# Reordering four places of a hand-written schedule: a crossbar transpose, a scaling, a key transpose and a Strassen sum

## The chip, the core and the metric

The kernel runs on one core of a Trainium2 chip. The metric is the device time of one execution in microseconds (us); lower is better. One profiled execution gives the trace that all the durations below come from.

## What is computed

Eight batches go through causal attention with a sliding window of 64 positions, and the result goes through a layer norm and a two-layer feed-forward block with a residual connection. Cut to what matters:

```python
q, k, v: (8 batches, 8 heads, 576 positions, 64)  float32
scores = q @ k.T / 8;  mask: 0 <= pos_q - pos_k < 64
attn   = softmax(scores);  x = attn @ v        # (8, 576, 512), heads side by side
xn = (x - mean(x)) / sqrt(var(x) + 1e-6) * g_ln
out = x + relu(xn @ w_ch1) @ w_ch2             # w_ch1 512x2048, w_ch2 2048x512
```

## The kernel before

**Groups.** Each of groups 0 to 7 takes the first 512 positions of one batch; group 8 takes the last 64 positions of all eight. A group's 512 rows are four blocks of 128. In the names, `(g, kb)` is block `kb` of batch or group `g`.

**The feed-forward part of a group** is a list of *units* (`mlp_units`), run in order. Group 1 and group 2 begin with 16 units of the first layer in halves (`l1_half`, PSUM tile `hph`, L634): units 0 to 7 make columns 0 to 255 and read blocks 0 and 1 of the transposed input `zT`, units 8 to 15 make columns 256 to 511 and read blocks 2 and 3. Each unit's result leaves PSUM by a Relu on ScalarE (ACT, L639), and the pool `mm` that holds it has two banks. Then come 14 units of the second layer, in the Winograd form of Strassen's algorithm: seven products on TensorE (PE, L567), in the order 4, 1, 2, 6, 5, 7, 3, two units each, accumulated in the banks `pA`, `pB` and `pC`. The sums that the products read (`s_sums`, tiles `sS`, L541) and the adds of finished banks to the residual `xn` (`post`, L576 and L580) run on VectorE (DVE). Groups 3 to 7 take the first layer at full width (`hps`, L493).

**The next batch's attention** is laid between these units by hand. `at(i, f, ...)` puts a step into slot `i`, which runs after unit `i`; steps of one slot run in the order in which they were put there:

```python
for i, u in enumerate(units):
    u()
    for f, a in slots[i]:
        f(*a)
```

The program order decides everything: each engine and each DMA queue works through its own instructions in this order, and waits only for data, for a buffer, or for a place among the DMAs in flight.

**Steps that the change and the prediction touch**, in the order in which a block meets them:
- `cast_qk`, `cast_v` (L154, L182): float32 to half precision on GpSimd (POOL).
- `t_main(b, x, half)`: transposes q (`x` = 0) or k (`x` = 1) into `qkT`. For batch 2 by TensorE (L276), with the result copied out of PSUM by ScalarE (q, L257) or VectorE (k, L259). From batch 3 on, q goes by a DMA transpose through the crossbar on the sync queue (SP, L265).
- `part_vB`: two DMAs on SP that lay the value rows out a second time, shifted by 64 rows, after `cast_v`.
- `s_pe`, `s_exp`, `s_mask`: scores on TensorE (L349), exponentials on ScalarE (L359), mask on VectorE (L369). `first_scores(b, i)` puts those of blocks 0 and 1 in slots `i` to `i + 2`. `half` of `t_main` is heads 0 to 3 or 4 to 7.
- `b_pe`: probabilities times values on TensorE (L396). `b_rows`: reciprocal, product, statistics and aggregate on VectorE (L412, L416, L418, L421).
- `z_step`: the reciprocal root of the variance and the shifted mean, three small GpSimd instructions (L440 to L442). From group 3 on a fourth GpSimd instruction scales the block (L446); for batches 1 and 2 `z_act` (ScalarE, L452) or `z_dve` (VectorE, L456) does that later.
- `zt_step(g, kb)`: transposes the scaled block into `zT`. For batch 1 by TensorE (L470) with a ScalarE copy (L473), from batch 2 on by a DMA transpose on SP (L466).
- `load_qk`, `load_v`, `load_tail` (L92, L176, L104 to L106) load the batch after next and the tails; `store` (L528) writes results. All are on SP.

Of the kernel before, what the change touches and what calls it, by code (L numbers as in the profile page):

```python
# [13 lines left out]
ALU = mybir.AluOpType  # L14
# [4 lines left out]
def kernel(  # L19
# [10 lines left out]
    nc = tc.nc  # L30
# [49 lines left out]
    x_norm, zT, mvg, zsd, rstd = {}, {}, {}, {}, {}  # L80
# [367 lines left out]
    rsnm = {}  # L448

    def z_act(g, kb):  # L450
        rs, nm = rsnm[(g, kb)]
        nc.scalar.activation(out=zsd[(g, kb)], in_=x_norm[(g, kb // 2)][:, kb % 2, :], func=AF.Identity,  # L452
                             bias=nm, scale=rs)

    def z_dve(g, kb):
        nc.vector.tensor_scalar(out=zsd[(g, kb)], in0=x_norm[(g, kb // 2)][:, kb % 2, :],  # L456
                                scalar1=mvg[g][:, kb, 0:1], scalar2=rsnm[(g, kb)][0],
                                op0=ALU.subtract, op1=ALU.mult)
# [379 lines left out]
    for i in range(8):  # L838
# [8 lines left out]
        out=mask[0:64], in_=mask[0:64], compare_op=ALU.is_gt, fill=0.0,  # L847
# [3 lines left out]
        out=mask[64:128], in_=mask[64:128], compare_op=ALU.is_ge, fill=0.0,  # L851
# [87 lines left out]
    for g in range(NGRP):  # L939
# [4 lines left out]
        units, s_sums = mlp_units(g, (8, 16, 16)[g] if g < 3 else 0, g == 0, g > 0)  # L944
        slots = [[] for _ in range(len(units) + 1)]

        def at(i, f, *a):
            slots[min(i, len(slots) - 1)].append((f, a))

        def first_scores(b, i):  # L950
            at(i, s_pe, b, 0)
            at(i, s_pe, b, 1, False, "xps")
            at(i, s_exp, b, 0, 0, 1)
            at(i + 1, s_exp, b, 1, 0, 1)
            at(i + 1, s_mask, b, 0)
            at(i + 2, s_mask, b, 1)

        b = g + 1
        if g == 0:
# [19 lines left out]
            at(22, z_step, 1, 0)  # L979
            at(22, cast_act, 1, 0, 1)  # L980
            at(22, z_act, 1, 0)
            at(22, cast_qk, 1, 1, (1,))
            at(22, load_qk, 2, 1)
# [21 lines left out]
        if g == 1:  # L1005
            at(0, cast_qk, 2, 0, (0,))
            at(0, after_mask, 1, 3)
            at(0, cast_qk, 2, 0, (1,))
            at(0, cast_qk, 2, 1, (0,))
            at(0, alloc_v, 2)  # L1010
            at(0, alloc_qkT, 2)
            at(1, t_main, 2, 0, 0)
            at(1, b_pe, 1, 2, "t")
            at(1, b_pe, 1, 3, "sc")
            at(1, b_rows, 1, 2)
            at(1, z_step, 1, 2)
            at(1, cast_qk, 2, 1, (1,))
            at(1, b_rows, 1, 3)
            at(1, z_step, 1, 3)
            at(2, z_dve, 1, 2)  # L1020
            at(3, t_main, 2, 1, 0)
            at(4, t_main, 2, 0, 1)
            at(4, z_dve, 1, 3)
            for c in (0, 2):
                at(4, cast_v, 2, c, c + 2)
                at(5, part_vB, 2, c)
            at(5, zt_step, 1, 2)
            at(5, t_main, 2, 1, 1)
            at(6, zt_step, 1, 3)
            for n, i in enumerate((3, 2, 4)):  # L1030
                at(7, w2_sums, i, 4, 8)
            at(8, s_pe, 2, 0)
            at(8, s_pe, 2, 1, False, "xps")
            at(8, s_exp, 2, 0, 0, 1)
            at(9, s_mask, 2, 0)
            at(9, w2_sums, 1, 0, 8)
            at(10, s_exp, 2, 1, 0)
            at(11, s_exp, 2, 1, 1)
            at(12, s_sums, 0, 4, 1, 2)
            at(12, s_mask, 2, 1)  # L1040
            at(16, s_sums, 4, 8, 1, 2)
            at(20, s_sums, 0, 8, 3)
            at(24, s_sums, 0, 8, 4)
            for j in range(4):
                i = (13, 16, 22, 22)[j]
                at(i, b_pe, 2, j, "sc" if j == 3 else "xps")
                if j < 2:
                    at(i, s_mm, 2, j + 2)
                    at(19, s_mask, 2, j + 2)
                i = (13, 17, 23, 26)[j]  # L1050
                at(i, b_rows, 2, j)
                at(i, z_step, 2, j)
                if j < 3:
                    at((17, 20, 26)[j], z_act, 2, j)
                    at((17, 20, 26)[j], zt_step, 2, j)
            at(6, load_qk, 3, 0)
            at(8, load_qk, 3, 1)
            at(10, load_v, 3, 0, 4)
            at(8, alloc_qkT, 3)
            at(8, cast_qk, 3, 0)  # L1060
            at(14, cast_qk, 3, 1, (0,))
            at(17, cast_qk, 3, 1, (1,))
            at(18, alloc_v, 3)
            at(18, cast_v, 3, 0, 2)
            at(18, cast_v, 3, 2, 4)
            at(21, part_vB, 3, 0, 4)
            first_scores(3, 28)
            for i, (x, half) in zip((12, 21, 18, 24), ((0, 0), (1, 0), (0, 1), (1, 1))):
                at(i, t_main, 3, x, half, 0)
        if g == 2:  # L1070
            at(2, z_act, 2, 3)
            at(3, zt_step, 2, 3)
            at(3, load_qk, 4, 0)
            at(3, load_qk, 4, 1)
            at(3, load_v, 4, 0, 2)
        if g > 1 and b < B:
            tail = TAILS.get(g)
            at(2, b_pe, b, 0)
            at(2, b_rows, b, 0)
            at(2, z_step, b, 0)  # L1080
            at(2, s_pe, b, 2)
            at(2, s_exp, b, 2, 0, 1)
            at(3, s_mask, b, 2)
            if tail:
                r, i = NGRP - 1, tail[0]
                at(2, s_pe, r, i, False, "t")
                at(4, s_exp, r, i, 0)
                at(5, s_exp, r, i, 1)
                at(5, s_mask, r, i)
                at(7, b_pe, b, 1)  # L1090
                at(7, b_pe, r, i, "t")
                at(7, s_mm, b, 3)
                at(7, b_rows, b, 1)
                at(7, z_step, b, 1)
                at(8, s_mask, b, 3)
                at(8, b_rows, r, i)
                at(9, z_step, r, i)
                at(12, b_pe, b, 2)
                at(12, b_pe, b, 3, "sc")
                at(16, zt_step, r, i)  # L1100
            else:
                at(2, s_pe, b, 3, False, "t")
                at(4, s_exp, b, 3, 0)
                at(5, s_exp, b, 3, 1)
                at(5, s_mask, b, 3)
                at(7, b_pe, b, 1)
                at(7, b_pe, b, 2, "t")
                at(7, b_pe, b, 3, "sc")
                at(7, b_rows, b, 1)
                at(7, z_step, b, 1)  # L1110
            if g + 2 < B:
                at(5, alloc_qkT, g + 2)
                at(5, after_mask, *((NGRP - 1, tail[0]) if tail else (b, 3)))
                at(5, cast_qk, g + 2, 0)
                at(5, cast_qk, g + 2, 1, (0,))
                at(11, cast_qk, g + 2, 1, (1,))
            for j, i in ((2, 8 if g == 2 else 12), (3, 10 if g == 2 else 19)):
                at(i, b_rows, b, j)
                at(i, z_step, b, j)
            for j in range(4):  # L1120
                at((2, 14, 18, {3: 25, 5: 25}.get(b, 23))[j], zt_step, b, j)
        for n, i in enumerate(TAILS.get(g, ()) if b >= B else ()):
            ts = (13, 13, 17, 22) if n else (1, 2, 5, 11)
            at(ts[0], s_mm, NGRP - 1, i)
# [84 lines left out]
```

## Time and profile before

| | |
|---|---|
| time, median of 3 runs (lowest to highest) | 308.82 us (308.58 to 309.03) |
| the profiled execution | 308.97 us |
| its span | 307.2 us |
| TensorE busy | 292.8 us (95%) |
| VectorE busy | 220.1 us (72%) |
| GpSimd busy | 163.4 us (53%) |
| ScalarE busy | 154.7 us (50%) |
| 16 DMA engines, mean share of SP's queue | 78.7% |

How to read the views: a timeline line gives start, length, engine, source line, operation, output and inputs, how often, and in brackets the idle time before it with what ended it. A line of waits names the waiting engine and its source line, then what released it, then the total, the number and the longest. The chain of waits is the work that ended last, followed back step by step. PEld is TensorE's weight load, and `SPq` is an instruction of the sync queue that issues a DMA. In this execution group 1 begins at 53.6 us, group 2 at 88.8 and group 3 at 127.9.

### The profile page before, as it was taken

To read this page: it belongs to the slowest core of one execution; us is meant where nothing else is said; L and a number is where in the kernel's file an instruction comes from. 1 tells how busy PE (TensorE), PEld (TensorE's weight loads), DVE (VectorE), ACT (ScalarE), POOL (GpSimd) and SP (SyncE) were. 2 spreads that over 40 slices of the span, in tenths; PEclk is the share of its full clock that TensorE was granted. 3 is DMA by queue.
4 is the path that set the end of the run, shared out by engine and by line. 5 is a ranking of instruction groups with operands and counts; after the bars stand their busy time and mean duration, and the time that the engine had idled before them with its cause. 6 is when DMAs were issued, how large, how long until landed. Compare 5 with 4: busy or idle time off the path is not lost.

```text
span 307.2 us, 7809 instructions
## 1 busy us (share of the span) xinstructions
PE 292.8 (95%) x3179; PEld 207.1 (67%) x3179; DVE 220.1 (72%) x413; ACT 154.7 (50%) x260; POOL 163.4 (53%) x243
## 2 busy tenths in 40 slices
PE   8989999999997797999999999999999999999993
PEld 3657545888876686655975597559755864688882
DVE  3880387989986492459956985599558876689982
ACT  3566637686457342686247626862476046405500
POOL 4678887735833289059914963499127607024300
PEclk9999999999999799999999999999999999999999
DMA  8999999969943899799669998994629398003014
GB/s 189 262 385 337 388 280 294 267 204 302 143 123 113 250 221 170 202 316 202 94 178 321 175 197 234 316 152 100 135 101 188 70 168 209 17 19 139 1 36 104
DMA packets 114311, 58.36 MB, mean 190 GB/s; under 512 B 83682, under 2 KB 105250, under 8 KB 114275
## 3 DMA queue, kind: packets, MB, share of 16 engines
q1 hardware_dynamic: 113840, 57.47, 78.7%
q8 instruction: 25, 0.41, 0.6%
q10 hardware_dynamic: 434, 0.40, 0.4%
q14 instruction: 12, 0.09, 0.1%
HBM read 38.80 MB, written 9.44 MB: 157 GB/s over the span
## 4 chain that ended last, share of the span: by engine, by line
PE 77%; DVE 8%; SPq 6%; DMA 4%; POOL 2%; issue 1%; ACT 1%; DVEq 0%; POOLq 0%
PE hps L493 25%; PE pA L567 11%; PE pB L567 8%; PE pC L567 7%; PE hph L634 6%; PE ch L651 3%; PE xps L396 3%; PE sc L349 3%; SPq L176 2%; PE lA L690 2%; PE warm L861 2%; PE tp L276 2%; DVE xn L416 2%; DVE stats L418 2%; DMA tk<-in_k_dram 1%
## 5 line engine op out<-in xcount | busy, mean ns | idle before, releaser
L493 PE MATMUL hps<-zT,w1g 128*128 128x512 f16 x352 | 80.2, 379 | 0.4 <-DMA zT<-z 0.4
L497 ACT ACTIVATE hrT<-hps 128x512 f16<-128x512 f32 x88 | 52.8, 600 | 37.3 <-PE hps L493 34.2
L493 PEld LDWEIGHTS <-w1g 128*128 128x128 f16 x352 | 33.1, 98 | 38.6 <-issue 1.7
L567 PEld LDWEIGHTS <-sS 128*128 128x128 f16 x512 | 49.4, 98 | 6.2 <-issue 0.5
L359 ACT ACTIVATE pt<-sc 128x512 f16<-128x512 f32 x72 | 39.3, 601 | 20.3 <-PE sc L349 19.7
L440 POOL TENSOR_SCALAR rsz<-mvg 128x1 f32<-128x1 f32 x32 | 11.2, 350 | 66.3 <-DVE mvg L421 59.1
L634 PE MATMUL hph<-zT,w1g 128*128 128x256 f16 x320 | 39.3, 280 | 3.6 <-DMA zT<-z 3.5
L154 POOL CAST qk<-qk 128x1024 f16<-128x1024 f32 x29 | 32.7, 1142 | 16.6 <-DMA qk<-in_q_dram 14.3
L567 PEld LDWEIGHTS <-hrT 128*128 128x128 f16 x384 | 36.7, 98 | 7.0 <-ACT hrT L497 0.8
L634 PEld LDWEIGHTS <-w1g 128*128 128x128 f16 x320 | 31.3, 100 | 8.8 <-DMA zT<-z 3.6
L369 DVE TENSOR_TENSOR pt<-pt,mask 128x1024 f16<-128x1024 f16 x32 | 23.7, 748 | 17.9 <-ACT pt L359 17.9
L639 ACT ACTIVATE hrT<-hph 128x512 f16<-128x512 f32 x40 | 23.9, 599 | 16.2 <-PE hph L634 16.0
L541 DVE TENSOR_TENSOR sS<-hrT 128x1024 f16<-128x1024 f16 (+2 forms) x41 | 26.6, 648 | 7.1 <-ACT hrT L639 5.2
L567 PE MATMUL pC<-w2s,sS 128*128 128x256 f16 x256 | 31.1, 273 | 0.3 <-DVE xn L580 0.3
L567 PE MATMUL pA<-wT,sS 128*128 128x256 f16 x256 | 30.9, 273 | 0.0
L257 ACT COPY qkT<-tp 128x1024 f16<-128x1024 f16 (+1 forms) x18 | 17.3, 962 | 25.0 <-PE tp L276 23.2
L416 DVE TENSOR_TENSOR xn<-xps,rcp 128x256 f32<-128x256 f32 (+1 forms) x50 | 25.8, 539 | 2.4 <-DMA out_dram<-xn 1.6
L418 DVE BATCH_NORM_STATS2 stats<-xn 128x6 f32<-128x512 f32 x36 | 25.0, 695 | 1.2
L446 POOL TENSOR_SCALAR z<-xn,rsz 128x512 f16<-128x512 f32 x24 | 22.2, 927 | 2.5
L441 POOL TENSOR_TENSOR rsz<-rsz,mhalf 128x1 f32<-128x1 f32 x32 | 20.6, 642 | 2.7
L182 POOL CAST vA<-v 128x1024 f16<-128x1024 f32 (+1 forms) x18 | 16.0, 906 | 4.4 <-DMA v<-in_v_dram 4.2
L396 PEld LDWEIGHTS <-pt 128*64 128x64 f16 x576 | 11.5, 110 | 9.1 <-issue 5.1
(120 smaller groups left out, 420.4 us busy)
## 6 DMA issues: line engine op xcount, KB each, us to landing
qk<-in_q_dram SPq DMA_DIRECT2D x16, 512.0 KB, 5.9
qk<-in_k_dram SPq DMA_DIRECT2D x16, 512.0 KB, 6.8
out_dram<-xn SPq DMA_DIRECT2D x32, 256.0 KB, 3.4
v<-in_v_dram SPq DMA_DIRECT2D x28, 256.0 KB, 6.6
w2s<-in_moe_w_ch_dram SPq DMA_DIRECT2D x9, 512.0 KB, 8.5
w1s<-in_moe_w_ch_dram SPq DMA_DIRECT2D x4, 512.0 KB, 7.2
tk<-in_k_dram SPq DMA_DIRECT2D x8, 256.0 KB, 4.8
tv<-in_v_dram SPq DMA_DIRECT2D x8, 256.0 KB, 5.1
```

Of the source, the lines that this page charges most:

```text
L154: nc.gpsimd.tensor_copy(out=dst[:, :].rearrange("p (a j) e d -> p a e j d", j=j), in_=t[:, :].rearrange("p (a e j d) -> p a e j d", e=2, j ...
L359: nc.scalar.activation(out=o, in_=i, func=AF.Exp, bias=0.0, scale=scale)
L369: nc.vector.tensor_tensor(out=ptv, in0=ptv, in1=mb, op=ALU.mult)
L416: nc.vector.tensor_tensor(out=xn[:, n * i:n * i + n], in0=xps[:, :, 0:D], in1=rcp_b, op=ALU.mult)
L418: nc.vector.bn_stats(out=stats, in_=xv)
L446: nc.gpsimd.tensor_scalar(out=z, in0=xv, scalar1=rs, scalar2=nm, op0=ALU.mult, op1=ALU.add)
L493: nc.tensor.matmul(out=hps, lhsT=w1g[:, kc, 128 * hc:128 * (hc + 1)], rhs=zT[g][:, kc, :], start=(kc == 0), stop=(kc == NKC - 1),)
L497: nc.scalar.activation(out=hrT[:, hc, :], in_=hps, func=AF.Relu, bias=0.0, scale=1.0)
L541: nc.vector.tensor_tensor(out=o, in0=x, in1=y, op=op)
L567: nc.tensor.matmul(out=o, lhsT=a[:, c, 128 * p:128 * p + 128], rhs=wv[:, c, :], start=(first and (p == 0 or split_c) and c == 0), stop=(c ...
L634: nc.tensor.matmul(out=hps[:, e], lhsT=w1g[:, kc, 128 * hc:128 * (hc + 1)], rhs=zT[g][:, kc, 256 * half:256 * half + 256], start=(kc == 0) ...
L639: nc.scalar.activation(out=hrT[:, 2 * i:2 * i + 2, 256 * half:256 * half + 256], in_=hps, func=AF.Relu, bias=0.0, scale=1.0)
```

## The change

Four places in groups 1 and 2 move:

1. In group 2, batch 3's block 0 is transposed through the crossbar in slot 4 instead of slot 2, and batch 2's block 3 in slot 2 instead of slot 3. On the sync queue batch 2's block now stands ahead of batch 4's loads (four of q and k, four of v), and batch 3's block behind them and ahead of the tail loads. Before, batch 3's block came first, batch 2's second, and then the loads.
2. In group 1, batch 1's block 3 is scaled by a new step `z_pool` on GpSimd right after its small steps, where `z_dve` did it on VectorE in slot 4. The cast of the second half of batch 2's k, which stood on GpSimd between blocks 2 and 3, follows the scaling.
3. In group 1, TensorE's transposes of the second half of batch 2's k go from slot 5 to slot 8, directly ahead of batch 2's first scores. VectorE's copy of them goes behind the three w2 sums.
4. At the end of group 1, the fourth sum `sS` and the adds of product banks A and C come ahead of the value rows of batch 2's block 2 on VectorE, and batch 3's first scores on TensorE come behind both units of product 3 instead of between them.

ScalarE's order is the same as before. TensorE has the same instructions, VectorE one fewer and GpSimd one more.

```diff
+    def z_pool(g, kb):
+        rs, nm = rsnm[(g, kb)]
+        nc.gpsimd.tensor_scalar(out=zsd[(g, kb)], in0=x_norm[(g, kb // 2)][:, kb % 2, :], scalar1=rs, scalar2=nm,
+                                op0=ALU.mult, op1=ALU.add)
...
         if g == 1:
...
             at(1, z_step, 1, 2)
-            at(1, cast_qk, 2, 1, (1,))
             at(1, b_rows, 1, 3)
             at(1, z_step, 1, 3)
+            at(1, z_pool, 1, 3)
+            at(1, cast_qk, 2, 1, (1,))
             at(2, z_dve, 1, 2)
             at(3, t_main, 2, 1, 0)
             at(4, t_main, 2, 0, 1)
-            at(4, z_dve, 1, 3)
...
             at(5, zt_step, 1, 2)
-            at(5, t_main, 2, 1, 1)
             at(6, zt_step, 1, 3)
+            at(8, t_main, 2, 1, 1)
...
             at(8, s_pe, 2, 0)
...
-            at(24, s_sums, 0, 8, 4)
+            at(22, s_sums, 0, 8, 4)
...
-                i = (13, 17, 23, 26)[j]
+                i = (13, 17, 25, 25)[j]
                 at(i, b_rows, 2, j)
                 at(i, z_step, 2, j)
...
-            first_scores(3, 28)
+            first_scores(3, 29)
...
         if g == 2:
             at(2, z_act, 2, 3)
-            at(3, zt_step, 2, 3)
+            at(2, zt_step, 2, 3)
             at(3, load_qk, 4, 0)
...
             for j in range(4):
-                at((2, 14, 18, {3: 25, 5: 25}.get(b, 23))[j], zt_step, b, j)
+                at((4 if g == 2 else 2, 14, 18, {3: 25, 5: 25}.get(b, 23))[j], zt_step, b, j)
```

## The prediction, made before the changed kernel was run

> **What bounds the kernel now.** I read the page's busy shares first: TensorE (PE) is busy 292.8 of 307.2 us, so only its 14.4 us of idle time and any slow-clocked stretch are there to be won. Next I read the waits of TensorE alone between 50 and 130 us (waiting engine and line, releaser: total us, times, longest):
>
> ```profile
> PE hph L634 <- DMA zT<-z: 3.5, 1, 3.5
> PE tp L276 <- POOL qk L154: 1.8, 1, 1.8
> PE hps L493 <- DMA zT<-z: 0.4, 1, 0.4
> PE pC L567 <- DVE xn L580: 0.3, 1, 0.3
> PE ztp L470 <- DVE z L456: 0.3, 1, 0.3
> PE sc L349 <- DMA qkT<-qk: 0.2, 1, 0.2
> ```
>
> One wait stands out: group 2's half-width first-layer products (hph) stop for a transposed block zT. The timeline of all engines around it (start, length, what) shows why:
>
> ```profile
> 92.11 0.80 ACT L452 ACTIVATE z<-xn,rsz 128x512 f16<-128x512 f32 x1
> ...
> 96.75 1.20 POOL L446 TENSOR_SCALAR z<-xn,rsz 128x512 f16<-128x512 f32 x1
> ...
> 97.97 2.51 SPq L466 DMA_TRANSPOSE zT<-z  x2
> ...
> 100.54 0.57 SPq L92 DMA_DIRECT2D qk<-in_q_dram  x1
> ...
> 101.64 8.77 PE L634 MATMUL hph<-zT,w1g 128*128 128x256 f16 x64 [3.54 <-DMA zT<-z]
> ```
>
> Batch 2's last block is scaled on ScalarE by 92.91, but the sync queue (SP) first holds the transpose of batch 3's block 0, whose GpSimd scaling ends at 97.95. So batch 2's transpose issues at 99.27 and lands near 101.6, and batch 4's loads start only at 100.54. The stall costs more than its length, as hph's stages show (us; PE busy; ACT busy; granted clock; DMA share; GB/s):
>
> ```profile
> 98.10:101.64 3.54, 0.00 (x0) 0.00 (x0) 0.99 0.33 74
> 101.64:103.50 1.86, 1.86 (x9) 0.00 (x0) 0.50 0.79 189
> 103.50:105.20 1.70, 1.70 (x11) 0.60 (x1) 0.57 1.05 365
> 106.10:110.20 4.10, 4.10 (x40) 2.96 (x5) 1.00 1.20 302
> ```
>
> After the idle 3.54 us the clock is half for about 3.5 us. The 64 matmuls took 8.61 us to the next one's start at 110.25; at 1.75 per 16, as in group 1, they take 7.00. That is another 1.61.
>
> **The swap of the two transposes.** At 92.24 the queue has issued its four stores and is idle. With batch 2's block first, it issues right behind ScalarE: one transpose issue is 1.21, landing is 2.4 after the start. The stall would go, and batch 4's loads would move from 100.54 to about 92.95 + 1.21 + 0.06 = 94.2, or 6.3 earlier, if group 1 and the start of group 2 kept their times. They do not; that is the next two parts.
>
> Batch 3's block 0 now issues behind four qk and four v loads, still ahead of the tail loads. Its reader is group 3 at 127.9, so its own landing is harmless; the question is what its place costs the queue. Later groups have this order already (the sync queue's timeline):
>
> ```profile
> 160.85 0.46 SPq L92 DMA_DIRECT2D qk<-in_q_dram  x1
> ...
> 167.17 3.10 SPq L466 DMA_TRANSPOSE zT<-z  x1
> ...
> 178.76 3.84 SPq L265 DMA_TRANSPOSE qkT<-qk  x2
> ```
>
> There, first load to first qkT transpose is 17.91, with such a block inside; in group 2 the same eight plus six loads take 118.51 - 100.54 = 17.97 without one. Engines are full there (DMA share 1.05 from 101.6 to 110), so the issue hides in the backlog. I take 0, and 1.2 (one issue) as the other end.
>
> **Group 1: scaling on GpSimd, k's second half later.** The chain of waits carries this place:
>
> ```profile
> 61.90 1.19 DVE z L456
> ...
> 63.13 0.40 PE ztp L470 x4
> 63.53 1.75 PE hph L634 x16
> 65.28 0.57 PE sc L349 x32
> ...
> 84.59 1.11 DVE sS L541
> 85.70 0.60 DVE xn L580
> ```
>
> Now block 3's three small GpSimd steps start behind VectorE's aggregate (end 59.96, plus the 0.16 lag of block 2's), take 1.25 as at 60.57, and the scaling follows 0.1 later at 61.45. Its rows (L446) are 0.76 alone and 1.21 beside VectorE's half-precision sums; the three w2 sums (0.69 each) run from 61.9. So it ends at 62.2 to 62.7, against 63.08 on VectorE. TensorE, with the eight k transposes (0.45) taken out ahead, wants it at 62.2: it waits 0.3, the same as now. The longest such row, 2.17, would add 1.0.
>
> [...]
>
> The k transposes now stand directly ahead of batch 2's first scores, and those read what they produce: heads 0 to 3 are ready, heads 4 to 7 wait for VectorE's copy (1.21 for this tile) plus 0.2 from TensorE's end to VectorE's start and 0.05 back. The first eight of 32 score matmuls cover 0.57 / 4 = 0.14. New wait: 1.32. Queued behind it are the exponentials and the rest of half 1, and TensorE is then busy without a gap to 84 (6.00 of 6.00 in three stages), so nothing absorbs it. Call it 1.3 (1.1 to 2.3).
>
> GpSimd does batch 2's k and v casts about 1.7 later (z and cast order), and SP waits at 62.82 and 64.12 for them, so vB and batch 3's loads go 1.7 later, 0.4 more than TensorE does. The nearest one, batch 3's value cast, has no slack (its last load lands at about 83.1 and the cast starts then); what follows on GpSimd, block 2's small steps, comes 2.2 later anyway. I count 0. That VectorE loses a scaling (1.2) is worth 0: it then waits for TensorE.
>
> **End of group 1: the fourth sum and the C add ahead of the rows.** Gain: TensorE's 0.34 before the last C product goes, since VectorE's add of the first C product (end 84.11 on TensorE, plus 0.2, 0.6 long) is over at 84.9 while product 7 runs to 86.02. Cost: block 2's rows start at 84.9, not 82.72. They take 1.87, ending 86.8 instead of 84.59. GpSimd's small steps then take 1.35 (as for block 3; 2.2 as now beside the sum is the other end), so ScalarE scales block 2 at 88.13 instead of 86.79 and is done at 88.94. ScalarE runs in order: behind it queue batch 3's four exponentials (87.82 now, 2.06 long) and the first Relu of group 2 (89.90 now, releasing a bank at 90.50 that TensorE takes at 90.53 for its third product). The exponentials start at about 88.97, 1.15 later (1.1 to 2.0); the Relu and the third product follow. The scores, one slot later, pay only for 0.1: block 3's rows leave their bank at 87.85. From there ScalarE is the pace: 7.10 busy of 8.20 us between 90.0 and 98.2.
>
> **The sum.** Half 0 of group 2 runs 1.3 + 1.15 = 2.45 late (2.2 to 3.6). Block 3's scaling ends at 92.91 + 2.45 = 95.36, its transpose issues 95.4 to 96.6 and lands at 97.8, well before TensorE arrives at 100.55: no stall, full clock. TensorE is then 1.1 ahead of before, and 2.7 ahead after half 1. Batch 4's loads start at 96.65, 3.9 earlier. The next late thing is their chain. The cast of k's second half (ends 118.79 now, behind casts and scalings that the first landing at 105.19 starts) comes at 114.9, and TensorE wants it at 117.07 - 2.7 = 114.4: of the 1.8 wait, 0.5 stays. From there all three feeders, cast, qkT landing and zT landing (127.87 now), are 3.9 earlier, and group 3 starts 3.9 earlier. Later groups take their order from TensorE and shift whole. 308.97 (the profiled execution: span 307.2 and 1.77 around it) - 3.9 = 305.07; its run was 0.15 above the median of 308.82, so the forecast is **304.9**. Ends: -4.1 with the low costs, -3.9 + 1.15 + 1.2 = -1.5 with the high ones.
>
> **Rivals.** 0.2% is 0.62 us, about what a measurement of this kernel can tell from no change: 308.2 to 309.4 is the same.
> - *Forecast, loads pace group 3*: 304.6 to 307.3. Chance 0.62.
> - *More comes back*: the copy wait or the ScalarE lag is half as large (1.2 together), loads start 5.1 earlier, and TensorE's own sum allows it (3.54 + 1.61 + 1.8 + 0.4 + 0.2 - 1.2 = 6.3): 303.7. For it: ScalarE has gaps of 0.2 to 0.3 between Relus. Against: its next bank is taken 0.03 after release. 0.13.
> - *The price is paid twice*: GpSimd's scaling takes 2.2, block 2's small steps 2.2, and the block's issue 1.2: 307.3 to 309. The rows exist, but not all three together. 0.16, of which 0.09 still faster, 0.05 the same, 0.02 slower.
> - *Slower: the crossbar block dams the loads.* The longest L466 issue is 4.13 (137.0, behind loads) and the longest landing 6.8 against 4.0 at group 3's start. If that is time the queue loses, group 3 starts -3.9 + 4.1 + 2.8 = 3.0 later: 311.8. It decides from 3.9 up. Against: 17.91 beside 17.97. 0.07.
> - *The swap does not bite*, because the transpose waits for a landing of the stores (issued to 92.24, about 3.0 to land): it would issue at 95.2, where it stands anyway. 0.02, the same.
>
> Faster 0.62 + 0.13 + 0.09 = 0.84; same 0.05 + 0.02 = 0.07; slower 0.02 + 0.07 = 0.09. The range 303.5 to 307.6 leaves out the slow rival and most of the double price.
>
> **What would show it.** Right: no hph wait on zT; granted clock 1.00 through half 1 of group 2; TensorE waiting 1.2 to 1.4 for a VectorE copy at batch 2's first scores, and for a Relu at the third hph of group 2; batch 4's first load between 96 and 97.5; 17.9 from it to the first qkT. Wrong: a load start after 98.5, a new clock drop, or more than 19 from load to qkT.

## The result, and the profile after

| | median (lowest to highest), us | runs |
|---|---|---|
| after | 305.78 (304.71 to 307.57) | 11 |
| before, beside it on the same chip | 308.93 (308.58 to 309.85) | 11 |
| ratio | 0.9908, 95% interval [0.9884, 0.9933] | |

The kernel is 3.15 us faster where 3.9 was forecast. The profiled execution took 307.27 (span 305.5), 1.5 above the median: after spreads over 2.9 us where before, beside it, spreads over 1.3 (in a later set of 29 runs before spreads over 3.6 too). So this trace is read for mechanisms, and sizes are taken from a second profile of the same kernel too (the run `d_again` below, 306.37).

The waits of TensorE between 50 and 130 us, after:

```profile
PE tp L276 <- POOL qk L154: 2.8, 1, 2.8
PE sc L349 <- DVE qkT L259: 1.1, 1, 1.1
PE hph L639 <- ACT hrT L644: 0.6, 1, 0.6
PE ztp L475 <- POOL z L457: 0.6, 1, 0.6
PE hph L639 <- DVE xn L581: 0.4, 1, 0.4
PE hps L498 <- DMA zT<-z: 0.3, 1, 0.3
```

The 3.5 us on zT is gone, and the 0.3 of the C product. Four of the lines that stand there now were made by the change: the copy ahead of the scores (1.1), the Relu (0.6), an add of `post` (0.4), and a scaling that is 0.3 later for the block transposes. The top line was 1.8 before and was to shrink to 0.5; it grew to 2.8.

TensorE's stretches that stand where before was slow (start to end, length, busy time of PE, PEld, VectorE, ScalarE and GpSimd, granted clock, DMA share, GB/s):

```profile
95.27:100.84 5.57, 5.53 (x94) 4.68 (x89) 3.21 (x7) 5.16 (x10) 2.64 (x5) 1.00 0.78 251
100.84:107.84 7.00, 7.00 (x69) 6.28 (x65) 6.76 (x17) 4.18 (x7) 3.20 (x5) 1.00 1.00 278
```

Half 1 of group 2 runs at clock 1.00, and its 64 matmuls take the forecast 7.00 us instead of 8.61.

The sync queue, after:

```profile
95.74 1.23 SPq L471 DMA_TRANSPOSE zT<-z  x1
97.03 0.57 SPq L92 DMA_DIRECT2D qk<-in_q_dram  x1
...
99.93 8.98 SPq L176 DMA_DIRECT2D v<-in_v_dram  x4
109.02 2.48 SPq L471 DMA_TRANSPOSE zT<-z  x1
...
116.69 4.11 SPq L265 DMA_TRANSPOSE qkT<-qk  x2
```

Batch 2's block stands ahead of the loads and batch 3's block behind them, as the change says. The loads start 3.51 earlier than before (4.15, if one allows for the 0.64 by which this execution is late already at 60 us, ahead of every changed instruction; below, a *net* figure allows for it). But from the first load to the first qkT transpose it is now 19.66, not 17.97.

### The profile page after: what moved, and what is told of

Same layout as the page of the kernel before. It is cut to its first block, busy times and chain, and to the rows that moved or that the text cites. A ratio compares the mean times of both kernels' runs of the same rounds, so it can differ in the third digit from the quotient of the medians.

```text
span 305.5 us, 7808 instructions
## 1 busy us (share of the span) xinstructions
PE 291.7 (95%) x3179; PEld 206.6 (68%) x3179; DVE 217.3 (71%) x412; ACT 154.5 (51%) x260; POOL 165.2 (54%) x244
## 4 chain that ended last, share of the span: by engine, by line
PE 72%; DMA 12%; POOL 5%; SPq 3%; DVE 3%; ACT 2%; issue 1%; POOLq 0%; ACTq 0%
PE hps L498 23%; PE pA L572 12%; PE pB L572 8%; PE pC L572 8%; DMA qk<-in_k_dram 6%; PE hph L639 4%; PE xps L396 3%; PE sc L349 3%; DMA qk<-in_q_dram 3%; PE lA L695 2%; PE warm L866 2%; PE tp L276 2%; DMA tk<-in_k_dram 2%; DMA zT<-z 1%; ACT pt L359 1%
## 5 line engine op out<-in xcount | busy, mean ns | idle before, releaser
L498 PEld LDWEIGHTS <-w1g 128*128 128x128 f16 x352 | 33.1, 98 | 38.5 <-issue 1.7
L440 POOL TENSOR_SCALAR rsz<-mvg 128x1 f32<-128x1 f32 x32 | 10.7, 333 | 65.3 <-DVE mvg L421 55.9
L639 PE MATMUL hph<-zT,w1g 128*128 128x256 f16 x320 | 38.0, 273 | 1.1 <-ACT hrT L644 0.6
L639 PEld LDWEIGHTS <-w1g 128*128 128x128 f16 x320 | 30.4, 98 | 5.8 <-issue 1.6
L644 ACT ACTIVATE hrT<-hph 128x512 f16<-128x512 f32 x40 | 23.9, 600 | 10.7 <-PE hph L639 10.4
```

Of the source, the lines that this page charges most:

```text
L498: nc.tensor.matmul(out=hps, lhsT=w1g[:, kc, 128 * hc:128 * (hc + 1)], rhs=zT[g][:, kc, :], start=(kc == 0), stop=(kc == NKC - 1),)
L639: nc.tensor.matmul(out=hps[:, e], lhsT=w1g[:, kc, 128 * hc:128 * (hc + 1)], rhs=zT[g][:, kc, 256 * half:256 * half + 256], start=(kc == 0) ...
L644: nc.scalar.activation(out=hrT[:, 2 * i:2 * i + 2, 256 * half:256 * half + 256], in_=hps, func=AF.Relu, bias=0.0, scale=1.0)
```

## The experiments

**Theory.** The swap of the transposes earns all there is, and more than the whole change (4 to 6 us alone); the group 1 edits and the sums cost about 1 each; what is missing from the forecast is TensorE's wait for the cast of k's second half. **Rivals:** the edits in group 1 are worth something after all; batch 3's block behind the loads holds the queue up; the spread, not the median, carries the shortfall. Where several kernels were run together they share the runs of before: median 308.53 (29 runs) for the first four, 308.38 (15) for the next four, 308.71 (11) for the two after those.

| run | what it is | median, us | ratio to before [95%] |
|---|---|---|---|
| a_swap | edit 1 alone | 304.01 | 0.9861 [0.983, 0.9892] |
| b_group1 | edits 2 and 3 alone | 310.14 | 1.0053 [1.0031, 1.0074] |
| c_sums | edit 4 alone | 309.46 | 1.0033 [1.0013, 1.0053] |
| d_again | after, unchanged | 306.05 | 0.9911 [0.9885, 0.9936] |
| e_cast | a_swap, cast of k's second half early | 303.38 | 0.9821 [0.9796, 0.9847] |
| f_copy7 | after, k transposes one slot earlier | 304.99 | 0.9886 [0.9856, 0.9916] |
| g_z0late | a_swap, batch 3's block behind the tails | 310.11 | 1.0042 [1.0023, 1.0062] |
| h_zpool5 | edit 2 alone, k transposes in their old slot | 311.91 | 1.0098 [1.0068, 1.0127] |
| i_after_cast | after, with the early cast | 306.23 | 0.9907 [0.988, 0.9935] |
| j_qkt | e_cast, qkT transposes ahead of the tails | 303.77 | 0.983 [0.9811, 0.985] |

TensorE's timeline in the profiles shows that nothing behind group 2 matters: from group 3 on every group has the same length within 0.15 us in all of these kernels. Group 0, which no edit touches, varies by 0.8 us from profile to profile. Lengths (start to start, us):

| | before | after | d_again | a_swap | b_group1 | c_sums | e_cast | i_after_cast |
|---|---|---|---|---|---|---|---|---|
| group 1 | 35.32 | 36.20 | 36.21 | 35.27 | 36.72 | 34.76 | 35.37 | 36.21 |
| group 2 | 39.13 | 36.11 | 35.29 | 35.04 | 38.35 | 39.66 | 33.26 | 33.70 |

### The swap alone (a_swap)

```diff
-            at(3, zt_step, 2, 3)
+            at(2, zt_step, 2, 3)
...
-                at((2, 14, 18, {3: 25, 5: 25}.get(b, 23))[j], zt_step, b, j)
+                at((4 if g == 2 else 2, 14, 18, {3: 25, 5: 25}.get(b, 23))[j], zt_step, b, j)
```

> Only the two crossbar transposes change places (batch 2's block 3 ahead of batch 4's loads, batch 3's block 0 behind them); groups 1 and its end are as in the kernel before. Theory (the swap earns, the edits in group 1 and the sums cost): batch 4's first load moves from 100.54 to about 94.2, no wait of hph on zT, granted clock 1.00 after it, group 3 starts 4.6 to 6.3 earlier than before (4.6 if the loads take 1.7 longer, as in the changed kernel's trace): 302.6 to 304.2 us, below the changed kernel. Rival (the other edits are needed to let the swap work): some wait in group 1 or at the scores of batch 3 keeps it at or above the changed kernel's 305.8.

Measured: 304.01, 4.5 below before and 2.0 below the whole change beside it. Its loads start at 94.25, where the prediction had put them for the swap alone (94.2). The rest of the gain is held by one wait, seen in TensorE's timeline (idle time and its end in brackets):

```profile
114.06 0.62 PE L276 MATMUL tp<-ident,qk 128*128 128x128 f16 x8 [2.15 <-POOL qk L154]
114.52 1.55 PE L567 MATMUL pA<-wT,sS 128*128 128x256 f16 x8
115.87 3.10 PE L567 MATMUL pC<-w2s,sS 128*128 128x256 f16 x16
```

The 16 C products take 2.94 us from start to start instead of 1.75. Windows of the profile say why (the column before the last two is the granted clock):

```profile
114.20:116.20 2.00, 2.00 (x18) 1.57 (x17) 0.09 (x1) 1.01 (x1) 2.00 (x4) 0.67 1.79 199
116.20:118.20 2.00, 2.00 (x11) 1.36 (x10) 0.60 (x1) 0.00 (x0) 2.00 (x3) 0.50 0.94 190
```

So behind a wait of 2.15 us the half clock is back that the swap had removed at its old place.

### The group 1 edits alone (b_group1), the sums alone (c_sums), the change again (d_again)

b_group1 holds the hunks of edits 2 and 3 as they stand in the diff of the change, c_sums those of edit 4.

> Only the edits in group 1's first half: the scaling on GpSimd and k's second transposes ahead of the scores; the crossbar order is as before. Theory: a new wait of 1.1 to 1.3 of TensorE for VectorE's copy at batch 2's first scores, and group 2 starts 1.3 later; the 3.5 us wait on zT stays: 309.9 to 310.4 us. Rival (the scaling on GpSimd frees VectorE and pays for the wait): 308.5 to 309.2 us, no change.

> Only the fourth sum, the two product adds and the first scores at the end of group 1. Theory: the 0.34 wait of the last C product goes, but ScalarE scales batch 2's block 2 later, so that its exponentials and the first Relu of group 2 come 1.0 to 1.2 later and TensorE waits for them; the wait on zT gets shorter by part of that, since batch 3's block 0 hangs on the stores and shifts by only 0.6: 309.3 to 310.0 us. Rival (it pays for itself): 308.3 to 308.8 us.

> The changed kernel once more, unchanged. Its eleven times lie between 304.7 and 307.6 us, wider than those of the kernel before. Theory: the time of an execution follows how long batch 4's third load takes to land (8.4 us in the profiled execution of 307.27, 6.4 in the kernel before), since GpSimd's casts and with them a TensorE transpose wait for it; an execution near 305 shows a landing near 6.4 and a wait on the cast near 0.8 instead of 2.8. Rival: the spread comes from TensorE's clock after a wait of about 3 us, and the fast and slow executions have the same landings.

Measured: b_group1 +1.6 and c_sums +0.9 against before, so by the medians both parts cost. The longest waits of b_group1:

```profile
PE hph L639 <- DMA zT<-z: 3.0, 1, 3.0
PE tp L276 <- POOL qk L154: 1.8, 1, 1.8
PE sc L349 <- DVE qkT L259: 1.1, 1, 1.1
```

With the old order of the transposes the zT wait stands at 3.0, though what comes before it in group 1 has moved, and the copy wait is added. In c_sums the hph waits for the Relu and the add, known from after, show without the rest:

```profile
PE hph L634 <- DMA zT<-z: 2.9, 1, 2.9
PE tp L276 <- POOL qk L154: 2.0, 1, 2.0
PE hph L634 <- ACT hrT L639: 0.6, 1, 0.6
PE hph L634 <- DVE xn L576: 0.4, 1, 0.4
```

c_sums makes group 1 0.56 shorter (34.76 against 35.32), a little more than its 0.34 wait; it gives that back in group 2, where the waits for the add and the Relu are new. The profiles hold less of these costs than the medians: groups 1 and 2 together are 0.6 longer than in before in b_group1, and no longer in c_sums (74.42 for 74.45). Where c_sums loses its 0.9 no trace shows. The three parts sum to -4.5 + 1.6 + 0.9 = -2.0, and the whole change is at -2.5 beside them: they act nearly one by one. d_again repeats the result; its cast wait is 1.8, and its group 2 0.8 shorter than in the first profile of after, with the third cast 8.14 behind the first load for 9.65 there. That is the theory's direction; no execution near 305, where the theory would be tested, was profiled. The clock has a part in the spread too: of the 23 times of after in the two sets six lie above 307, and five of these have a mean granted clock of 0.992 to 0.994, where none of the others is below 0.995.

### Is the cast wait the missing part? (e_cast, i_after_cast, and that again twice)

e_cast is a_swap with one more line, i_after_cast is after with that line alone:

```diff
-                at(11, cast_qk, g + 2, 1, (1,))
+                at(5 if g == 2 else 11, cast_qk, g + 2, 1, (1,))
```

> The swap alone, and in group 2 the cast of the second half of batch 4's k on GpSimd right behind the other three casts (slot 5 instead of 11), ahead of the scalings. Theory (after the swap, TensorE's wait of 2.2 us for this cast, and a clock drop of 1.7 us that sometimes follows it, set the time): the wait on GpSimd is gone, no clock below 1.00 between 108 and 124, the next limits are the landings of qkT and zT, which TensorE waits for with 1 to 2.7 us in all; group 3 starts near 122.9 instead of 123.9; 302.9 to 303.9 us, and the times lie closer together than 2 us. Rival (the wait only moves on and the scalings, 1.0 later, make zT land later too): 304.0 to 304.8 us.

> The changed kernel with the cast of the second half of batch 4's k right behind the other three (slot 5 instead of 11), and nothing else. The changed kernel's times spread over 304.7 to 307.8 us. Theory (the spread is TensorE's wait for that cast, 1.8 to 2.8, and the clock drop that sometimes follows it): the wait on GpSimd is gone, the times lie within 1.5 us of each other, median 304.4 to 305.4 us. Rival (the spread is in the landings themselves): it stays over 2 us wide, with the same median of 305.8 to 306.1 us.

Measured: e_cast 303.38, the fastest of all and 5.0 below before. Its cast wait is gone, the clock is 1.00 from 114.0 to 118.0, where a_swap has 0.72 and 0.50 in the two halves of that stretch, and the next feeders are what is late:

```profile
PE sc L349 <- DMA qkT<-qk: 1.3, 2, 0.8
PE hps L493 <- DMA zT<-z: 0.4, 1, 0.4
```

On the base of a_swap the theory holds in the trace (group 2 is 1.8 shorter); by the medians the gain is 0.6, and the two intervals overlap. On the base of after it only half does: i_after_cast's profiled execution has no cast wait and took 304.45, but its median is 306.23 (304.45 to 307.20), no better than after. So the cast wait isn't what spreads this kernel. It was profiled twice more, in k_again1 and k_again2:

> The changed kernel with the early cast, once more, for a second profile: its six times lay between 304.5 and 307.2 us, so the wait for the cast was not the spread. Its first profile (304.45) has 33.7 us from group 2's start to group 3's and no clock below 1.00. Theory now (a clock drop after a short wait, of 1.6 us, in group 1 or 2, or both): an execution above 306 shows granted clock near 0.5 for some 3 us in groups 1 or 2, and that group is longer by 1.5 to 1.8. Rival (landings): group 2 is longer with the clock at 1.00 and a longer wait for qkT or zT.

> The same kernel a third time, for the same question: above 306 us with a clock drop of 1.6 us in group 1 or 2 by the theory, with longer waits for landings and the clock at 1.00 by the rival; near 304.5 us it tells only that the fast execution repeats.

They took 305.53 and 305.35, with clock 1.00 from 56 to 124 and group 2 at 34.62 and 34.42 (33.70 in the quicker profile). First load to qkT was 18.78 and 18.21 (17.80 there), and TensorE's qkT wait 1.6 and 1.1 (0.7). In these three profiles, 304.45 to 305.53, the time follows the landings of the loads. No execution of this kernel above 306 was profiled. Its two longest runs, 306.88 and 307.20, have a mean granted clock of 0.992 and 0.991 where the other four have 1.00, so a lower clock has a part in those two; the run of 306.45 has none, and what makes it longer is open.

### The copy ahead of the scores (f_copy7, h_zpool5)

f_copy7 is after with one line moved:

```diff
-            at(8, t_main, 2, 1, 1)
+            at(7, t_main, 2, 1, 1)
```

> The changed kernel with the k transposes in slot 7 instead of 8: one hph unit (0.87) lies between them and the scores. Theory (the wait for VectorE's copy is 1.1 of the loss in group 1, and it reaches the loads through ScalarE): the wait for the copy is below 0.3, perhaps 0.3 for the cast instead, batch 4's loads start 0.7 to 1.1 earlier than in the changed kernel (95.7 to 96.3): 304.8 to 305.5 us. Rival (the loads do not hang on it): 306.0 us as the changed kernel.

Measured: 304.99. The copy wait is 0.2 instead of 1.1, and the loads start at 95.24 instead of 96.75 (d_again) or 97.03. With this wait mended, after is still not below a_swap (304.01); the intervals of the two overlap, so which is faster isn't shown.

h_zpool5 takes the GpSimd scaling into before and leaves the k transposes in slot 5:

> The kernel before with the scaling on GpSimd only; the k transposes stay in slot 5. Theory (GpSimd, in order, hands over the k cast 2.7 to 4 us later than before): TensorE waits 2 to 3.5 us on the cast at the k transposes, more than the 1.1 of slot 8, and group 2 starts 2 to 3 later: 310.3 to 311.5 us. Rival (the cast is early enough): 308.5 to 309.2 us.

Measured: 311.91, the slowest of all.

```profile
PE tp L276 <- POOL qk L154: 4.1, 2, 2.1
PE hph L639 <- DMA zT<-z: 2.6, 1, 2.6
```

Two waits of about 2 for casts, one more than before: the k cast now stands behind the scaling on GpSimd. The new wait also brings half clock (TensorE's timeline):

```profile
63.33 0.62 PE L276 MATMUL tp<-ident,qk 128*128 128x128 f16 x8 [2.03 <-POOL qk L154]
63.78 1.59 PE L639 MATMUL hph<-zT,w1g 128*128 128x256 f16 x8
```

The granted clock is 0.50 from 64.1 to 67.5: these 8 matmuls take 1.39 us from start to start and the next 16 take 2.78, where full clock gives 0.88 and 1.75. Group 1 is 3.2 longer than in before. So edit 3 is what edit 2 makes necessary; together they cost 1.6, edit 2 alone 3.5.

### Batch 3's block, and the queue's order (g_z0late, j_qkt)

g_z0late is a_swap with `5 if g == 2` in place of `4 if g == 2`: the block's transpose stands behind the tail loads.

> The swap alone, with batch 3's block 0 transposed in slot 5 instead of 4, behind the tail loads too. Theory (its place among the loads costs the queue its own issue, 1.7, and nothing else): the tail loads issue 1.7 earlier after the first load (10.7 to 11.0 instead of 12.5), the qkT transposes as before at 18.4; the third k/q landing and the cast wait stay, and so does the time: 303.6 to 304.4 us. Rival (the block makes the loads around it land later): the third cast starts 7.6 after the first load as in the kernel before, not 8.3, and the time falls below 303.5.

Measured: 310.11; both the theory and the rival said a time near a_swap's. GpSimd's timeline shows what both had left out:

```profile
111.56 0.27 POOL L442 TENSOR_SCALAR rsz<-mvg,rsz 128x1 f32<-128x1 f32 x1
117.01 0.77 POOL L446 TENSOR_SCALAR z<-xn,rsz 128x512 f16<-128x512 f32 x1 [5.19 <-DMA zT<-z]
117.72 1.04 POOL L154 CAST qk<-qk 128x1024 f16<-128x1024 f32 x1
```

The pool of scaled blocks has three buffers. Block 3's scaling needs the one that block 0's transpose reads, and waits 5.19 for that transpose to land; the cast stands behind it, and TensorE waits 6.8 for the cast, with the mean granted clock at 0.51 from 114.20 to 116.20 and 0.50 from 116 to 120. In a_swap block 0's transpose issues at 104.99 for a scaling at 112.26, in after at 109.02 for one at 115.62: its place there is harmless only because it lands before that scaling. On the rival, that the block makes the loads around it land later, the third cast doesn't decide: it starts 7.9 behind the first load, where before has 7.6 and a_swap 8.35. But the eight loads take 10.9 to issue without the block behind them, as in a_swap with it (10.7), so the block isn't what holds up their issue.

j_qkt is e_cast with the qkT transposes in slot 5 and the tail loads in slot 6:

```diff
-            for i, (x, half) in zip((13, 18, 13, 22) if g == 2 else (13, 17, 13, 21),
+            for i, (x, half) in zip((5, 18, 5, 22) if g == 2 else (13, 17, 13, 21),
...
-                at(4, load_tail, i)
+                at(6 if g == 2 else 4, load_tail, i)
```

> The swap with the early cast, and on the sync queue the two qkT transposes of batch 4 ahead of the tail loads instead of behind them. Theory (TensorE's last waits there are 1.3 for qkT and 0.4 for zT; the queue's total is the same): the wait for qkT goes, the tail loads land 3 to 4 later and TensorE waits up to 1 for their cast, zT lands as before: 302.6 to 303.4 us, 0 to 0.8 below the swap with the early cast. Rival (the tails become the bound): 303.8 to 305 us.

Measured: 303.77, against 303.38 of e_cast. The qkT waits are gone; a zT wait of 1.5 ahead of group 3 and a wait of 0.7 for a tail cast stand in their place. Changing the order of these transfers moved the wait and earned nothing.

## Why the prediction was right, and where its steps were not

**The swap: right in mechanism and size.** No zT wait, clock 1.00 in half 1, 8.61 to 7.00 for its matmuls; with the swap alone, loads at 94.25 for 94.2.

**Group 1's first half: right.** Batch 2's next unit behind the scores starts at 67.74, not 65.78; less the 0.64 of this execution that is 1.32 for 1.3. The waits were 1.10 for the copy and 0.6 (for 0.3) for the scaling. GpSimd's timeline of after:

```profile
62.11 1.21 POOL L457 TENSOR_SCALAR z<-xn,rsz 128x512 f16<-128x512 f32 x1
63.27 1.48 POOL L154 CAST qk<-qk 128x1024 f16<-128x1024 f32 x1
64.70 1.50 POOL L182 CAST vA<-v_tk 128x1024 f16<-128x1024 f32 x1
```

The scaling took the row's 1.21, beside VectorE's first sum, which ran from 61.99 to 62.67. What the prediction left out is the casts behind it, 1.48 and 1.50 instead of 1.04, and the two later sums beside them, 1.15 and 1.41 instead of 0.69: longer on both engines, off TensorE's path. Batch 3's loads issue 3.39 later (68.74 for 65.35), 2.75 net, where 1.7 was said; TensorE has no wait from that, as was said.

**End of group 1: right, with one wait not foreseen.** The 0.34 is gone. ScalarE's timeline of after:

```profile
90.05 0.81 ACT L452 ACTIVATE z<-xn,rsz 128x512 f16<-128x512 f32 x1 [3.65 <-POOL rsz L442]
90.77 2.04 ACT L359 ACTIVATE pt<-sc 128x512 f16<-128x512 f32 x4
...
94.91 0.81 ACT L452 ACTIVATE z<-xn,rsz 128x512 f16<-128x512 f32 x1
```

The exponentials start 2.95 later than before; without the 0.64 and the 1.32 that is 1.0, for 1.15. The Relu wait at the third hph came as said (0.6). The 0.4 wait for an add at the second was not in the prediction. Block 3's scaling is 2.80 later, or 2.16 net, for 2.45 (before has the two rows at 87.82 and 92.11).

**The step that failed: from the loads to group 3.** The loads came 3.5 earlier (4.15 net) where 3.9 was forecast, and then the chain did not shift whole, as the prediction had it ("all three feeders ... are 3.9 earlier"). The rows of GpSimd after:

```profile
102.22 1.04 POOL L154 CAST qk<-qk 128x1024 f16<-128x1024 f32 x1 [1.33 <-DMA qk<-in_q_dram]
105.17 1.04 POOL L154 CAST qk<-qk 128x1024 f16<-128x1024 f32 x1 [1.91 <-DMA qk<-in_k_dram]
106.68 1.04 POOL L154 CAST qk<-qk 128x1024 f16<-128x1024 f32 x1 [0.47 <-DMA qk<-in_q_dram]
...
116.33 1.04 POOL L154 CAST qk<-qk 128x1024 f16<-128x1024 f32 x1
```

Measured from the first load's issue (us, one profile each):

| | before | b_group1 | c_sums | a_swap | d_again | after |
|---|---|---|---|---|---|---|
| third cast starts | 7.57 | 7.49 | 7.80 | 8.35 | 8.14 | 9.65 |
| eight loads issued | 10.0 | 9.9 | 10.2 | 10.7 | 11.2 | 12.0 |
| fourth cast starts | 17.21 | 16.97 | 17.46 | 18.72 | 18.36 | 19.30 |
| first qkT transpose issues | 17.97 | 17.54 | 17.37 | 18.43 | 19.19 | 19.66 |

In these three profiles of the swapped order the third cast starts 0.6 to 2.1 later than in before and the loads take 0.7 to 2.0 longer to issue, both before the block's transpose is reached on the queue. The second holds in every profile (10.7 to 12.0 in the swapped order, 9.9 to 10.5 in the old one); the first doesn't (7.70 in f_copy7, 8.15 in h_zpool5, which has the old order). That transpose then takes 1.7 to 2.5 of issue, but the tail loads behind it are quicker by about as much (5.2 to 6.3 from the first one to the qkT transpose, against 7.2 to 8.0). The term taken as 0 (other end 1.2) measured 0.5 to 1.7 at the qkT transpose and 1.2 to 2.1 at the fourth cast, against before, so the cast wait stayed at 1.8 to 2.8 instead of 0.5. The prediction's own mark for being wrong, more than 19 from load to qkT, was passed in both profiles of after. So groups 1 and 2 together are 2.1 (after) and 3.0 us (d_again) shorter than before, where 3.9 was forecast. The median still came within 1 us because this term cost about 1 to 2 us, the other terms came within 0.4 us, and the dam of 4.1 + 2.8, the slow rival, did not come. Why loads that issue 4 to 6 us earlier take longer was not settled. One candidate was only argued: they now come 2 us behind the four result stores, where before they came some 8 us behind them.

**A step that held for another reason than the one given.** "Its own landing is harmless" named the reader in group 3; g_z0late shows a second one, the buffer for block 3's scaling, at a price of about 6 us against a_swap.

**The signs of the edits.** That edits 2 to 4 cost more than they give stands in the prediction's sum (2.45 for half 0, against 0.34), and the medians confirm it: the swap alone would have been the better change (304.01 against 306.05 in d_again, on the same chip), and with the early cast better by 2.4 us (303.38 against 305.78, from different chips; 0.9821 against 0.9908 of before).

## What to carry to other kernels

When a stall is taken out of a rigid schedule, shift every feeder behind it separately: here the transfers that started earlier did not land earlier by as much. Split a bundle of edits and price each: here one of four edits earned 4.5 us and the others gave about half of it back. And before a DMA is moved later, look for everything that waits for its source buffer, not only for the reader of its result.

## What the runs showed of the hardware that was not expected

The clock fell at waits much shorter than the 3.54 of before: in a_swap it fell to 0.50 behind 2.15 us of idle time, 0.8 us after the work went on, for 3.4 us (114.9 to 118.3, an estimate from the windows above and the matmul rows), at a cost of about 1.7 us (8 matmuls in 1.35 for 0.88, and 16 in 2.94 for 1.75). In h_zpool5 it fell behind 2.03 and again behind 2.06 us. In after 2.76 us of idle time left it at 1.00, and it is 1.00 from 117.43 to 121.43 too:

```profile
114.67:117.43 2.76, 0.00 (x1) 0.01 (x1) 0.00 (x0) 0.00 (x0) 2.56 (x5) 1.00 1.28 219
```

So in these profiles the length of the wait alone does not decide: 2.03 to 2.15 us were enough in h_zpool5 and a_swap, and 2.76 us were not in after. What else decides these runs do not show.

While a value load's issue was held on the sync queue in after, the DMA engines were nearly idle:

```profile
107.03:109.03 2.00, 2.00 (x19) 1.62 (x18) 2.00 (x3) 1.19 (x2) 1.83 (x3) 1.00 0.28 59
```

A mean DMA share of 0.28 and 59 GB/s, in the middle of a queue that had more to send. Before has 1.32 and 236 GB/s at the corresponding place (108.50 to 110.50). What holds the queue there is open.
